# Eight array tiles and two PSUM pairs for the first step of an inverse transform, absolute phases on ScalarE, a joined table product, and a new order of all pieces

## The chip, the cores and the metric

The kernel runs on one core of a Trainium2 chip. The core has a matrix engine (TensorE, in the profile PE for the matmuls and PEld for the loads of weights), a vector engine (VectorE, DVE), a scalar engine (ScalarE, ACT), a general engine (GpSimd, POOL) and a queue that issues transfers (SyncE, SP). Each engine takes its own instructions strictly in the order in which the program lists them, and waits on semaphores for the others. TensorE writes its results to PSUM, from where ScalarE or VectorE must take them away before the place is used again; this is called evacuation here. The metric is the device time of one execution in microseconds (us), lower is better.

## What is computed

Two independent parts, whose results stand side by side in the output (2048 rows, 576 columns each):

```python
def _A_ref(x, wqkv, wo):                # sliding-window attention, 32 heads of 18, window 256
    qkv = (x @ wqkv).reshape(B, S, 3, H, Dh).transpose(2, 0, 3, 1, 4)
    q, k, v = qkv[0], qkv[1], qkv[2]
    scores = jnp.einsum("bhqd,bhkd->bhqk", q, k) * (Dh ** -0.5)
    mask = (idx[:, None] - idx[None, :] >= 0) & (idx[:, None] - idx[None, :] < W)
    p = _softmax(jnp.where(mask[None, None], scores, -1e9), axis=-1)
    return jnp.einsum("bhqk,bhkd->bhqd", p, v).transpose(0, 2, 1, 3).reshape(B, S, D) @ wo

def _B_ref(u, A_re, A_im, B_re, B_im, C_re, C_im, log_dt, Dskip):   # state-space convolution
    dt = jnp.exp(log_dt)[:, None]
    P = jnp.exp((dt * A)[:, :, None] * l[None, None, :])            # A = A_re + 1j A_im, 128 states
    K = jnp.einsum("dn,dnl,dn->dl", Cc, P, dt * Bc).real            # 2048 taps for each of 576 channels
    Yf = rfft2(pad(u)) * rfft2(pad(K))                              # transforms of length 4096
    return irfft2(Yf)[..., :L] + u * Dskip
return jnp.concatenate([a, b], axis=-1)
```

## The kernel before

**Stages.** The front loads x and the weights, scales them, splits each into a high and a low half-precision part and starts the projections. The tables stage computes, for 18 groups of 32 channels, the factors of exp(dt A l) from exponentials and sines, multiplies them into two tables (P and Q) and forms the taps K from these on TensorE (L615), then K's first transform step (L631, L635) and u's (L493); the projections to q, k and v (L204) run between these. Then come the attention of 16 items (4 blocks of rows by 4 groups of heads) and the convolution's remaining steps side by side, and at the end the output product with wo.

**Pieces and their order.** The work is cut into pieces, each a stream that a letter names. A string of letters for each stage, `PLAN`, sets the order of the pieces; a letter with a digit is the follow-up of a piece (an evacuation, a store). Nothing is rescheduled after that: each engine gets its instructions in the order in which the pieces are written. The letters that matter here are G (factors and phases to PSUM, L505, and folding them, L511 and L514), N (sines), R (products for P, on GpSimd), M (exponentials and Q), X (taps), P (projections), s (score blocks whose maxima VectorE takes, L906, L914 and L940), a (scores for the softmax, L982, and their exponential, L1000), v (product with V, L1020), c (spectra of the convolution, L718), d (the first step of the inverse transform, L752), e (its last step, L815) and w (output product).

**The ring.** PSUM has three places of two banks each, the ring pairs. Most pieces on TensorE take one, c takes two, v none (it has its own, `po`). A second string, `SLOTS`, says which pair comes next. A piece that takes a pair waits until the evacuation of its last user is done, and so does everything behind it in TensorE's queue.

**Inverse, first step.** 24 steps (3 channel groups by 8). Each has 16 fp32 matmuls of 32 rows, 64 columns of weights and 192 streamed columns; the trace counts two for each, 768 in all. b numbers four row groups of 32. Row group b writes to column half b % 2 of one pair, so four different tiles of the array are used in turn. One ScalarE instruction (L759) evacuates the pair, two stores of 128 partitions bring it to `h` in DRAM, from where the last step (L815) reads it once eight inverses are done.

**Phases.** `fold` subtracts from a phase its whole part (L514) and, with an integer AND on VectorE (L515), writes its absolute value beside it, for the cosine. `t_sin` takes sine and cosine on ScalarE (L556, L557, L561, L562). `t_q` forms Q by four VectorE products of 512 elements (L601 to L604).

Of the kernel before, what the change touches and what calls it, by code (L numbers as in the profile page):

```python
# [29 lines left out]
HC = GC // 2  # L30
# [12 lines left out]
def constants():  # L43
# [23 lines left out]
    for nm, v in mult.items():  # L67
# [25 lines left out]
        "P2U4X1XMGPMGX5G5RP1PG6M1PP2X2PP4NRPP4RPMP1MG1PP2PM1UX4PP1XGRX1NP4XG2PP2GX1MG5UX4G5MPG6U2G6X4P4RU1U4R"
        "P1M1X4XX2PPXMRNU4P2GPX5P1X1MNRP2PXG1G2P4PGM1X1PG5PPXP5X4GPPP5RX5UMG5G6PG6UPPNU1UX2MRRPP4U2M1U4UU2XPP"
        "5MMRX1PGP5P6UG1U1PM1PPPG2P5UX4NRU1PMPMGM1XPP5PX1U2RU4G5P5GG5PPG6RMGXG6PP5PRX2NP6NP4PPG1MG2XPPGX5PRM1"
        "UP1G5P2P1MMGX1M1G5G6P2G6X4RXX4PPX1NXPPGP1X2PX5MGP4X4XG1RRP2MPX1PG5PNM1RG2G6XP1GX1PG5P1MMM1XG6X2P2X4P"
        "X4GPP4PRRP2P4NNMX5XG1RMP1M1G2PP4PX1UU1P2PRMGG5P1PGU4XU2P4G5UMG6P2PP6PUPG6X1X4PPM1XNU1RP1PGMP4PMPRX5P"
        "2U2G1RXPP1M1UNP4X1P5PXPGUX1PU1X2PG5X4P5GU4P2MRPU4G2MPPX4G5PP5U2XPG6PG6U4RP6M1PMNXP6GPPMRP4PGNRPRX5P5"
        "G1GPZX2X1G2M1P5P5PX4G5PPP5G5XX4X1MGUPG6G6PXRX5MPM1PP5X2PXNMPMPP1PP2X4PG1M1UX1PRU1RG2MP4NU2GP1UXUG5X1"
        "MPU1G6M1RP4U4P1GP2PPPUPG5U2XPPP2G6RNMP1RUX5PX4GPG1X4X2P1P4P2U2RUP4MP4NG2XM1X4RPU1GPX1G5P2MXP1GMX1G5G"  # L100
        "6P2PP4G6PPM1RPU4U4PMP4NP1XX4X4XMPZX2ZPM1UP2PURRX5NGX1MU1U2P1MXPPP1GPPP2X4PM1G1X1GP2PPG5XU4P6P5PP5X4P"
        "MG5G2G6UUX5PRRPPG6P6URU2MNXX2RU1PPP5P4GX4M1P5U2U1X1NG1MP4PMPXGP6M1PPP6P5PG2MPX4PRG5PGMPPP5X1G6P5XRXG"
        "5M1P4G6P6RsP5P6NU4sX2P6sU4sRMs2ss2ssX5ss2X4ssZs2s2sss2s2s2Zs2ZX1Ns2ss2sXs2s2X1ss2Rss2XZs2s",
    "first":
        "s6X5s4sX2s2sX4s2RMsss2M1saaRs2Xa1ssa1s2X1MRXs2X1sXX4saas2aX5sas2sX2X4sa1sa1s2vX4s2vs2a1ss2X4s2s2ss2s"
        "s2aavsa1sssa1s",
    "rest":
        "s6s2asssa1s2s2s2s4va1s2ssvs2akLs2svss2skss2vLvksa1sks2vvv1as2ala1s2s2s2sas2s2aa1svcvsaa1a1as6snsasvc"
        "1cac6a1s4s2ss2va1ks2a1kLas2c2ks2c1asva1vsa1asa1vlc3s2caa1s2vc2svc1ks2vs2saa1dscc6as2c2sa1kc3sv1d1vc1"
        "c6asa1kLLs2ln3s2s2c2dln1a1c3cs2anss2vsad4d1c1vs2Lka1sasa1avsc6n3ss6n6s2d4Lvskva1ac3vvs2s4sa1ks2ss2Lc"  # L110
        "6dLn1s2s2saa1vvasd1d4s2da1salsssac2a1ks2svd1Laa1sv1s2d4s2slvs2s2s2s2s2sc3s2a1csa1sLdlas6cvasvsac1d1k"
        "sa1c2vc6vs2asnsc1ks4aa1sn4a1vs2ss2a1vas2s2a1d4ka1svsc3Ln6s2n4s2as2svLs2dsas2sc2cs2as2La1sc6s2v1s2vd1"
        "a1n3c3sadsc1a1s2ad4a1c2c6c3vs2vd1aa1kdsaslsvvd4nsaa1sd1s6vsa1kLad4kn3s2ss2a1svs4sssa1vs2vcn1s2ss2s2L"
        "s2asn6ass2ac1a1va1ffa1ss2s2Las2s2Ls2ses2s2c6a1sc2av1ve1c3a1vks2skssds6e4an4n1svasas2vss2d1ls2ss2s2a1"
# [24 lines left out]
    "2101201201210210201210210210212012021020121020120120120210210210212010212012012012012021021012102102"  # L139
    "0102102102012012012010210210120120120210210201201201201210210201201201201201201201201201202102102101"  # L140
    "2012012010210210120120121021021021021021020120120120210120120102102102102102120120120120121200201201"
    "202010210210200210210212012"
)


# [1127 lines left out]
```

## Time and profile before

| | |
|---|---|
| Runs (us) | 786.18, 777.06, 781.0; median 781.0 |
| Profiled execution, first to last instruction | 784.5 us; its time is not listed apart from that |
| Mean granted TensorE clock | 0.963 |
| Busy, share of the span | PE 88%, DVE 75%, ACT 68%, POOL 53% |
| Front | 0 to about 53 us |
| Tables | to about 345 us, last taps end at 382.5 us |
| First inverse, last inverse | 421.0 us, 717.0 us |

A row of the profile that groups instructions reads: line, engine, operation, tiles out<-in, shapes, count | busy time in us, mean ns of one | idle time of the engine just before them, and what ended it. A row of waits reads: who <- for whom: us in total, times, longest. In the chain of waits a row is start, length, what. L752 is line 752 of the kernel before. A matmul's duration in the trace includes its way through the array, which the next one overlaps.

### The profile page before, as it was taken

What the parts mean: (1) busy time and instruction counts of PE and PEld (TensorE: products, weight loads), DVE (VectorE), ACT (ScalarE), POOL (GpSimd) and SP (SyncE); (2) the same over time, 40 slices, a digit from 0 to 9 for tenths busy, and PEclk for the clock granted to TensorE, in tenths of its full rate; (3) what the DMA queues carried; (4) which work ended last, traced back from release to release, by engine and by line L of the source; (5) the groups of instructions that cost most, each with busy time, mean ns of one, the idle gap of its engine ahead of it and who ended that gap; (6) DMA issues with size and microseconds to landing.
All of it is one profiled execution on the core that took longest, in us unless ns stands there. A gap on an engine that the chain in (4) does not pass through costs nothing.

```text
span 784.5 us, 29499 instructions
## 1 busy us (share of the span) xinstructions
PE 693.0 (88%) x12956; PEld 410.8 (52%) x12956; DVE 588.2 (75%) x779; ACT 534.3 (68%) x709; POOL 417.3 (53%) x309
## 2 busy tenths in 40 slices
PE   3786878998989989997789999989989998999997
PEld 2532444565545654665544555544555554557775
DVE  5998789998998897988777888876888586852100
ACT  2369577787887777773458677775877876786622
POOL 2245867987688666866007574451553444546120
PEclk9979799999999999996999999998999999899999
DMA  8998055738247537889578777676866786555786
GB/s 309 342 215 204 7 133 149 159 83 216 51 120 182 133 70 175 230 183 277 113 238 279 247 240 231 207 243 166 245 185 203 240 256 207 170 163 159 205 258 187
DMA packets 215904, 150.67 MB, mean 192 GB/s; under 512 B 103530, under 2 KB 195818, under 8 KB 215520
## 3 DMA queue, kind: packets, MB, share of 16 engines
q1 hardware_dynamic: 214160, 146.28, 66.0%
q0 software_dynamic: 1616, 2.52, 1.1%
q8 instruction: 101, 1.65, 0.8%
q14 instruction: 27, 0.22, 0.1%
HBM read 83.50 MB, written 65.11 MB: 189 GB/s over the span
## 4 chain that ended last, share of the span: by engine, by line
PE 55%; DVE 17%; ACT 15%; issue 6%; DMA 4%; SPq 1%; POOL 0%; ACTq 0%; DVEq 0%
PE po L1020 9%; PE pp L204 9%; PE ring L204 7%; PE ring L906 5%; DVE m L940 5%; PE ring L752 4%; PE ring L982 4%; PE ring L615 4%; PE ring L718 4%; PE ring L505 2%; DMA wraw<-in_wr_dram 2%; DVE amx L192 2%; PE ring L815 2%; ACT raw L1000 2%; DVE wl L372 2%
## 5 line engine op out<-in xcount | busy, mean ns | idle before, releaser
L940 DVE TENSOR_REDUCE m<-ring 128x2 f32<-128x640 f32 (+4 forms) x256 | 190.8, 779 | 66.0 <-PE ring L914 58.2
L586 POOL TENSOR_TENSOR m<-A,tr 128x1024 f32<-128x1024 f32 x72 | 141.5, 1983 | 52.6 <-DVE m L592 43.5
L1000 ACT ACTIVATE P<-ring,esc 128x1024 f32<-128x1024 f32 (+2 forms) x86 | 90.0, 1060 | 37.1 <-PE ring L995 32.7
L1000 ACT ACTIVATE raw<-ring,esc 128x1024 f32<-128x1024 f32 (+2 forms) x74 | 77.2, 1061 | 19.4 <-PE ring L995 18.8
L734 POOL TENSOR_TENSOR t<-X 128x768 f32<-128x768 f32 x24 | 46.7, 1944 | 76.1 <-ACT X L726 75.6
L1063 POOL TENSOR_TENSOR oh<-osb,oh 128x1024 f16<-128x1024 f32 x16 | 34.1, 2133 | 59.5 <-ACT oh L1059 42.9
L914 PE MATMUL ring<-sm,idb 64*64 64x128 bf16 x896 | 56.1, 224 | 3.3 <-issue 3.1
L204 PE MATMUL pp<-xh,wh 128*128 128x512 f16 x180 | 48.1, 397 | 10.0 <-DVE qst L453 5.0
L204 PEld LDWEIGHTS <-wh 128*128 128x128 f16 x324 | 30.7, 99 | 49.1 <-issue 11.7
L615 PE MATMUL ring<-Q,m 128*32 128x64 f32 x2304 | 42.9, 231 | 12.8 <-ACT fa L511 4.1
L1055 POOL TENSOR_TENSOR osb<-osb,T 128x1024 f32<-128x1024 f32 x16 | 38.6, 2410 | 25.8 <-DVE T L1050 23.8
L592 DVE TENSOR_TENSOR m<-m,m 128x1024 f32<-128x1024 f32 x36 | 51.6, 1432 | 0.7 <-POOL m L586 0.6
L615 PEld LDWEIGHTS ring<-Q,m 128*32 128x32 f32 x2304 | 36.9, 117 | 27.2 <-ACT mab L547 5.5
L906 PEld LDWEIGHTS <-raw 54*64 54x64 f16 x704 | 28.6, 108 | 41.1 <-issue 37.7
L740 POOL TENSOR_TENSOR Y<-t,t 128x384 f32<-128x384 f32 x24 | 24.7, 1029 | 46.1 <-DVE t L734 33.8
L906 PE MATMUL ring<-K,raw 54*64 54x320 f16 (+4 forms) x576 | 44.8, 308 | 4.5 <-ACT raw L1000 0.8
L204 PE MATMUL pp<-xh,wl 128*128 128x512 f16 x180 | 48.0, 400 | 0.6 <-DVE wl L372 0.6
L567 POOL TENSOR_TENSOR tr<-tr,mab 128x768 f32<-128x768 f32 x18 | 33.3, 1850 | 28.4 <-ACT tr L562 28.4
L726 ACT ACTIVATE X<-ring 128x768 f32<-128x768 f32 x48 | 36.7, 812 | 14.3 <-PE ring L718 8.1
L995 PE MATMUL ring<-tm,idb 64*64 64x256 bf16 (+2 forms) x640 | 45.0, 257 | 0.0
L982 PEld LDWEIGHTS <-K 55*64 55x64 f16 x1280 | 28.8, 108 | 26.7 <-issue 22.7
L752 PE MATMUL ring<-Y,i 32*64 32x192 f32 x768 | 38.7, 336 | 3.3 <-issue 2.3
(171 smaller groups left out, 1725.1 us busy)
## 6 DMA issues: line engine op xcount, KB each, us to landing
gk<-kst SPq DMA_DIRECT2D x36, 256.0 KB
gx<-ust SPq DMA_DIRECT2D x16, 576.0 KB
xk<-gx SPq DMA_DIRECT2D x24, 384.0 KB
xk<-gk SPq DMA_DIRECT2D x24, 384.0 KB
h<-ho SPq DMA_DIRECT2D x48, 192.0 KB
hp<-h SPq DMA_DIRECT2D x24, 384.0 KB
K<-kz SPq DMA_DIRECT2D x14, 512.0 KB
raw<-qz SPq DMA_DIRECT2D x11, 512.0 KB
```

The source lines that it names most:

```text
L204: self.nc.tensor.matmul(ps, u, v, start=(i == 0), stop=(i == len(ops) - 1))
L586: tt(m[part], A[:, ch, a0:a0 + 8].unsqueeze(3).to_broadcast(sh), tr[:, ch, part, 0:8].unsqueeze(2).to_broadcast(sh), op=OP.mult)
L592: self.nc.vector.tensor_tensor(m[0], m[0], m[1], op=OP.add)
L615: nc.tensor.matmul(kp[32 * st:32 * st + 32, j, :], m[:, ch, 32 * term:32 * term + 32], Q[:, ch, term, :], start=(term == 0), stop=(term == ...
L734: mul(ts[i], X[:, :, :, :192].rearrange("p i s j -> p s i j"), X[:, i, :, 192:].unsqueeze(2).to_broadcast(sh), op=OP.mult)
L752: nc.tensor.matmul(ps[64 * (b % 2):64 * (b % 2) + 64, b // 2, 192 * s:192 * s + 192], self.i1[32 * b:32 * b + 32, t, o:o + 64], Y[32 * b:3 ...
L906: nc.tensor.matmul(ps[z:z + 64, b, :n], d["Q"][rr, 2 * b + pp, 64 * qb:64 * qb + 64], d["K"][rr, 2 * b + pp, k0:k1], start=True, stop=Fals ...
L914: nc.tensor.matmul(out, self.idb[rr], self.sm[rr], start=False, stop=True, skip_group_check=True)
L940: self.nc.vector.tensor_reduce(out, x, axis=AX.X, op=OP.max)
L982: nc.tensor.matmul(ps[z:z + 64, b, off:off + w], d["K"][rr, 2 * b + pp, kc:kc + 64], d["Q"][rr, 2 * b + pp, q0:q0 + w], start=(k == 0), st ...
L1000: nc.scalar.activation(P[:, :, lo:hi], ps[:, :, lo:hi], AF.Exp, scale=self.esc)
L1020: nc.tensor.matmul(po[32 * p:32 * p + 32, z, q0:q0 + w], V[64 * z:64 * z + 64, kb * 76 + 19 * p:kb * 76 + 19 * p + 32], P[p % 2][64 * z:64 ...
```

## The change

Four edits. The first spreads the inverse's matmuls over eight tiles: the column half is now the transform's half s, the four row groups write to four banks, and so two ring pairs are taken; two ScalarE instructions evacuate them, and the two stores read 64 partitions each. The second takes the absolute value of a phase out of `fold` and lets ScalarE do it in `t_sin`. The third joins two of the four products of `t_q`. The fourth replaces all strings of `PLAN` and `SLOTS` (751 ring pairs instead of 727, one more for each inverse).

```diff
 PLAN = {
     "front":
-        "AAAVCACAAAAAVAVVV1CV1CAVAVAAVCAV1ACCVCACCVVV1VV1CVCACBBPABV1CCPV1BV1CPCPP1PVP2PP4CPAPP1PP2BPCP1P4BVP"
+        "AAAAAAAAAAAAAAAAACCCCCCCVCCCCVBVV1V1AVVVV1CV1CVVVBV1AVBBCV1CVCPCVV1PAV1CVCVBBC",
...
         def sub():
             nc.vector.tensor_tensor(k, x, k.bitcast(I32), op=OP.subtract)
-            nc.vector.tensor_scalar(f[:, 1].bitcast(I32), k.bitcast(I32), 0x7FFFFFFF, None, op0=OP.bitwise_and)
             self.n[end] += 1
...
             f = self.fr[c]
+            nc.scalar.activation(f[:, 1], f[:, 0], AF.Abs)
             nc.scalar.activation(f[:, 0], f[:, 0], AF.Sin, scale=-TWO_PI)
...
         v = lambda z: z.rearrange("p (c m) -> p c m", m=12)
+        nc.scalar.activation(f[:, 1], f[:, 0], AF.Abs)
         nc.scalar.activation(tr[:, :, 1, :], v(f[:, 0]), AF.Sin, scale=TWO_PI)
...
-        tt(Q[:, :, 0, 32:64], cs, m[:, :, 32:64], op=OP.mult)
+        tt(Q[:, :, :, 32:64], f.rearrange("p i (c m) -> p c i m", m=32)[:, :, ::-1],
+           m[:, :, 32:64].unsqueeze(2).to_broadcast([128, HC, 2, 32]), op=OP.mult)
         tt(Q[:, :, 0, 0:32], cs[:, :, ::-1], m[:, :, 0:32], op=OP.mult)
-        tt(Q[:, :, 1, 32:64], sn, m[:, :, 32:64], op=OP.mult)
...
     def inverse(self, n):
         nc, (ch, t), Y = self.nc, divmod(n, 8), self.Y.pop(n)
-        ps = self.slot()
-        for s in range(2):
-            for i in range(2):
-                for b in range(4):
+        ps = [self.slot() for _ in range(2)]
+        for i in range(2):
+            for b in range(4):
+                for s in range(2):
                     o = (2 * s + i) * 64
-                    nc.tensor.matmul(ps[64 * (b % 2):64 * (b % 2) + 64, b // 2, 192 * s:192 * s + 192],
-                                     self.i1[32 * b:32 * b + 32, t, o:o + 64], Y[32 * b:32 * b + 32, i, s],
-                                     start=(s == 0 and i == 0), stop=(i == 1), skip_group_check=True)
+                    nc.tensor.matmul(ps[b // 2][64 * s:64 * s + 64, b % 2, :192], self.i1[32 * b:32 * b + 32, t, o:o + 64],
+                                     Y[32 * b:32 * b + 32, i, s], start=(i == 0), stop=(i == 1), skip_group_check=True)
...
         def go():
-            ho = self.p["fs"].tile([128, 2, 2, 192], F32, name="ho")
-            nc.scalar.activation(ho.rearrange("p s b j -> p b s j"),
-                                 ps[:, :, :384].rearrange("p b (s j) -> p b s j", s=2), AF.Copy)
+            ho = self.p["fs"].tile([128, 4, 192], F32, name="ho")
+            for k in range(2):
+                nc.scalar.activation(ho[:, 2 * k:2 * k + 2], ps[k][:, :, :192], AF.Copy)
...
             for s in range(2):
-                nc.sync.dma_start(v[t, s], ho[:, s])
+                f = 8 * t + 4 * s
+                nc.sync.dma_start(self.h[f:f + 4, :, :, 192 * ch:192 * ch + 192].rearrange("b a l j -> (a l) b j"),
+                                  ho[64 * s:64 * s + 64])
...
-            yield "PE", lambda: (self.Y[n],), "ring", lambda: n in self.Y
+            yield "PE", lambda: (self.Y[n],), "ring", "ring", lambda: n in self.Y
             self.inverse(n)
```

Three places show the new order, in rows of the built program (line, operation, tile written <- tiles read, shape, count; lines from 180 to 600 stand one or two lower after the change). The first is on TensorE where an inverse is followed by a spectrum, ahead of the change:

```order
L914 LDWEIGHTS idb
L914 MATMUL ring<-sm,idb 64x2x64
L752 MATMUL ring<-Y,i_5189 64x192 x16
L718 MATMUL ring<-xk,w_5188 32x384 x16
L982 LDWEIGHTS K_4695
L982 MATMUL ring<-Q_4696,K_4695 64x256
```

and such a place after it:

```order
L995 LDWEIGHTS idb
L995 MATMUL ring<-tm,idb 64x128
L1020 MATMUL po<-P,raw 32x320 x8
L752 MATMUL ring<-Y,i_5231 64x192 x16
L718 MATMUL ring<-xk,w_5230 32x384 x16
L922 MATMUL ring<-idf,m 32x128
L906 LDWEIGHTS raw
```

The inverse has as many matmuls as before; a product with V (L1020), which takes no ring pair, stands ahead of it here and of ten others. Inverse and spectrum together now take four pairs, not three.

The second is ScalarE in the tables, around the first sines (fr and fa hold the phases, qst a projection, mab and ring exponentials), ahead of the change:

```order
L511 ACTIVATE fa<-ring 128x384
L527 ACTIVATE ring<-ring 128x1024
L511 ACTIVATE fr<-ring 128x512
L556 ACT_TABLE_LOAD
L556 ACTIVATE fr<-fr 128x512
L557 ACTIVATE fr<-fr,halfpi 128x512
```

and after it:

```order
L510 ACTIVATE fa<-ring 128x384
L449 ACTIVATE qst<-pp 128x512 x2
L525 ACTIVATE ring<-ring 128x1024
L510 ACTIVATE fr<-ring 128x512 x2
L554 ACTIVATE fr<-fr 128x512
L555 ACT_TABLE_LOAD
L555 ACTIVATE fr<-fr 128x512
L556 ACTIVATE fr<-fr,halfpi 128x512
```

The absolute value (L554) stands ahead of each pair of sine and cosine, and two evacuations of projections now stand ahead of the exponential.

The third is TensorE at the end of the tables, where the first score blocks (L906 and L917) run. Ahead of the change one block follows the other:

```order
L917 LDWEIGHTS idb
L917 MATMUL ring<-sm,idb 64x64
L906 LDWEIGHTS raw
L906 MATMUL ring<-raw 64x192
L906 LDWEIGHTS raw
```

and after it four matmuls of a projection to v (L203, in its own PSUM place pp) stand between two blocks here:

```order
L917 LDWEIGHTS idb
L917 MATMUL ring<-sm,idb 64x64
L203 LDWEIGHTS xl
L203 MATMUL pp<-wh,xl 128x288
L203 LDWEIGHTS xl
L203 MATMUL pp<-wh,xl 128x288
```

In all, 74 projection matmuls stand behind the first score block now, and none did.

More of the change, by code (lines that the diff above doesn't have):

```diff
@@ L93 @@
[L93 to L102, printed above, removed]
@@ new lines @@
+        "G1G2XX1GG5G6GG5G6NRMPPPM1MRX4X4X4U4NXX5X2UUP4P4P2U1U2UPU4XP1P4X1UMRRPU2X4X4PM1XX1P5P2PU1PMGPP5PG1G2X"
+        "GX5G5G6MPX2X4PM1UNRGP5G5P6MRPPPPPRX4G6UU2NP5P6P4XPX1RXP5PMM1MPU1PP5PX1PPGGGG5U4G6G1G2NG5G6PPXX2P5PPR"
+        "RMM1X5MMM1PPP5XNMMPP1P2RX1RGG1NPPPP1G2GG5RM1G6UXX1GMMPPG5G6XX2P6PP2PRXM1NX1RX5GNPMMP1P2GM1RG5G6PG1PP"
+        "4P4P1GG5G6P4X4X4P2PG2NXX1MPRPURU2PU1P1XP2XX4X4P4RX5X2X4RGG1P4NG2PMX1XM1X1GMP1P2MM1G5G6UPGG5G6NRRPPPP"
+        "1XP4X2PXPRMP1MP2X1PX5RM1UP2NPPP1U4U2U4GPPPX4X4G1MP5U1G2GGG5P2G5G6G6PRMM1RPPP5X4XX1P4MRPPPPPUUU2XX2NU"
@@ new lines @@
+        "1UU4U4P5X5PP5GG1XX1MM1G2PPPPP5MPGPPG5G6P6P5MM1PPGG5G6X4PRPP5X4PPXX1NRXX2NPX5MRPPUU1U2UUU2U4X4P5MM1XU"
+        "1RX1GRMGG5G6G1G2PGPP4P1P2G5PPG6P4P4UUU2NNUXX1U1PPXRU4U4RX2RP6UZP1X5P2ZU2RGG1G2PU1MM1MMXPX1PP1P2GGM1M"
+        "G5G6G5PPPMG6P4P4XP1P2PNRRRPP1P2ZZM1MX4X1XNX2PMP4PP4P1XX1X5X4RXGPPG1M1X4X1G2XX5MX2P1P6ZGG5P2P4GG5NRG6"
+        "G6MM1PPMPP2RUUU4NU1U2PPX4XP1X1X4RRUUU2U1GGP2MG1M1G2NX4X4PP1XX1G5PPMMM1PG6XRP2PPX5RP5XPX2P5MGPG5PX1RG"
+        "6ss2ss2Nsss2s2ss2P4sP4sP4s2s2U4U4Pss2sssP5s2Ps2Ps2ss2ss2PssPPPRP6P6P6P5P6s2s2MM1ss2MMPP5X4PXPM1MX1XP"
@@ new lines @@
+        "1saa1kvs2c2avva1aa1ss2cc1ss2s4asvva1ss2saa1vs2vks2ckc3v1c2c6LLkksc3s2c1ada1d1ndd1cc2c6c3sc1as2Lsss6v"
+        "d4a1s2ac2da1d4d1ss2ava1sasa1s2s2ks4aa1c6c3kLcc1c6ss2ss2kvss2aa1aa1c2vvc3vsss2cc1ss2ss2s2avla1dd1sc6a"
+        "vkc2ka1s2svs2sd4s2aLss2LLsn6vv1va1aa1s2ss6sLss2s2dd4d1ssss2s2s2csn3n1s2c1ac3c2a1c6aaa1ss2a1vaa1ss2av"
+        "sa1sks2s2akka1vvssc3s4s2aaa1a1sLs2Ls2ass2a1lcc1c6ss2vvc2dn6d1aLa1ss2aa1vc3sas6sss2d4va1s2ksaa1ss2s2s"
+        "s2vv1dd1kkdd4d1s4cd4c1nn3ss2aa1vd4ssc2vs2s2c6c3aa1svaa1s2ssvvan4n1s2s2a1ssvvn4s2s2ssaLLs2vsvs2s2aLa1"
@@ L139 @@
[L139 to L142, printed above, removed]
+    "0120201012010210212021201212012010202120212010210121122010210200120221021201212012102012010102111200"
+    "0122012012102001022120121011202102022101210121020212021002102010022021021012012002121021021021021021"
@@ new lines @@
+    "0212020120120120102102102102120121012012012012012012012102012010120120120120120120120120102102102010"
+    "2102102102102102102012012012102012102102102102102102101202102102102120212012012012012012012012102102"
+    "1202102102102102102102101201202102100210210210210210210120120120120120120210120121021021201202102102"
+    "1021210210210210210210120120120120120120210210201201202102102012012101201201201201201021201201201202"
+    "1021021012012102102010210210120120120120120120102102101201201201210210210212012102102120120102102021"
@@ L143 @@
+    "021021021010210210210102102101021021021021021020210"
 )
```

59 lines of the change are left out of this document (24 added, 35 removed).

## The prediction

> **What bounds the kernel now.** I read the page first (busy time, the chain of waits), then the busy time by stage, then the groups of the lines that the change touches.
>
> ```profile
> span 784.5 us, 29499 instructions
> ...
> PE 693.0 (88%) x12956; PEld 410.8 (52%) x12956; DVE 588.2 (75%) x779; ACT 534.3 (68%) x709; POOL 417.3 (53%) x309
> ...
> PE 55%; DVE 17%; ACT 15%; issue 6%; DMA 4%; SPq 1%; POOL 0%; ACTq 0%; DVEq 0%
> ```
>
> TensorE is busy 88% of the span, and it holds 55% of the chain that ended last; VectorE and ScalarE hold 17% and 15%. By stage (front, tables, the end of the tables, attention with convolution, the tail):
>
> ```profile
> core 0: us, PE busy (x) PEld busy (x) DVE busy (x) ACT busy (x) POOL busy (x), PEclk, DMA share, GB/s
> 0.00:53.00 53.00, 32.44 (x117) 18.36 (x118) 42.17 (x50) 19.91 (x26) 12.33 (x20) 0.90 0.92 300
> 53.00:345.00 292.00, 258.23 (x3382) 148.31 (x3381) 255.20 (x343) 226.75 (x360) 218.15 (x169) 0.97 0.58 140
> 345.00:402.00 57.00, 45.52 (x1051) 31.43 (x1058) 48.21 (x76) 25.43 (x39) 20.76 (x18) 0.85 0.75 196
> 402.00:700.00 298.00, 276.98 (x7336) 155.33 (x7321) 231.06 (x300) 225.15 (x243) 143.21 (x92) 0.98 0.73 222
> 700.00:784.50 84.50, 79.79 (x1082) 57.39 (x1080) 11.51 (x14) 37.04 (x44) 22.88 (x13) 1.00 0.64 196
> ```
>
> From 402 us on TensorE is the bound: 356.77 us busy of 382.5. What it no longer has to do there comes off the span, as long as nothing new makes it wait. In the tables (53 to 345) it is nearly level with VectorE, 258.23 against 255.20, and ScalarE is not far below with 226.75.
>
> **The inverse step (L752).** It removes no matmul; it spreads the same ones over eight array tiles instead of four. The neighbouring spectrum step (L718) already fills eight.
>
> ```profile
> L752 PE MATMUL ring<-Y,i 32*64 32x192 f32 x768 | 38.7, 336 | 3.3 <-issue 2.3 <-POOL oh L1063 0.4 <-DVE m L940 0.3
> L718 PE MATMUL ring<-xk,w 64*32 64x384 f32 x768 | 38.6, 487 | 0.8 <-DVE m L940 0.7
> ```
> ```profile
> L752 PE MATMUL ring<-Y,i x768: 317/321/576, 421.0 to 716.7; 32*64 32x192 f32 x192
> ```
> ```profile
> L718 PE MATMUL ring<-xk,w x768: 479/482/508, 406.5 to 708.6; 64*32 64x384 f32 x192
> ```
>
> Both have 768 matmuls and the same busy time (38.7 and 38.6 us), though those of L718 stream twice the columns: eight at once with 384 columns cost what four at once with 192 do. The medians give the streaming alone: 482 less 321 ns is 161 ns for 192 columns, so 160 ns of each matmul is latency. An inverse has 32 matmuls: eight waves of four now, 8 x 161 = 1.29 us and the latency; four waves of eight then, 0.64 us and the latency. That is 0.64 us less for each of 24 inverses, 15.5 us, all on TensorE after 402 us, where it is the bound. From below the price is nothing saved (the two column halves of one row group run one after the other); I take 15.5, since L718 runs eight tiles with four on the same rows.
>
> A row on small matmuls bears on this: 64 of them took 1.10 us here, 17 ns each, under the 20 ns that an inverse of 0.64 us needs.
>
> ```profile
> 167.39 1.10 PE ring L615 x64
> ```
>
> The Trainium skill, "TensorE: Matmul & The Clock Gate", section on the 56 ns gap, states that starts of matmuls never come closer than about 25 ns. By that an inverse would take 32 x 25 = 0.80 us and the 24 would save 11.8 us. The trace of this case does not agree (17 ns), so the row decides.
>
> **Its second PSUM pair.** The inverse now takes two of the three ring pairs and writes both at once, so it waits until the step before the last one has been evacuated. Nothing in the trace shows this step with two pairs; the nearest is L718, which takes two. Four waves of 2 x 161 ns and 160 ns of latency are 1.45 us; its busy time is 38.6 / 24 = 1.61, so about 0.16 us each is lost, 3.9 us in 24. From above the price is the whole gain, 15.5 us, since L718 fills its first pair for 0.64 us before it needs the second and the inverse does not; from below 0. I take 3.9: the new order puts matmuls of L1020, which need no ring pair, ahead of many inverses.
>
> Behind a waiting inverse stands all of TensorE's queue, score and projection matmuls alike, and behind those ScalarE and VectorE.
>
> **Its evacuation.**
>
> ```profile
> L759 ACT ACTIVATE ho<-ring 128x768 f32<-128x768 f32 x24 | 19.5, 811 | 16.7 <-PE ring L752 16.6
> ...
> L547 ACT ACTIVATE mab<-ring 128x384 f32<-128x384 f32 x18 | 8.8, 491 | 2.2 <-PE ring L505 2.1
> ```
>
> One evacuation of 811 ns becomes two of 128x384, by L547 491 ns each: 0.17 us more, 4.1 us in 24. ScalarE is busy 225.15 of 298 there and holds 15% of the chain: 0.6 us on the path (0 to 4.1). The stores to h stay 48 of 192 KB in SyncE's queue, from 64 partitions instead of 128: I cost that at nothing, because the reads of h come only after eight inverses of a channel group.
>
> **Absolute phases and the joined product, in the tables.**
>
> ```profile
> L592 DVE TENSOR_TENSOR m<-m,m 128x1024 f32<-128x1024 f32 x36 | 51.6, 1432 | 0.7 <-POOL m L586 0.6
> ...
> L515 DVE TENSOR_SCALAR fr<-fr 128x512 int32<-128x512 int32 x36 | 35.7, 992 | 1.2
> ...
> L601 DVE TENSOR_TENSOR Q<-fr,ring 128x512 f32<-128x512 f32 x36 | 24.5, 680 | 7.6 <-ACT ring L527 4.9 <-PE ring L615 2.0 <-ACT fr L557 0.7
> ...
> L556 ACT ACTIVATE fr<-fr 128x512 f32<-128x512 f32 x36 | 22.4, 623 | 0.4 <-DVE fr L515 0.2
> ...
> L515 DVE TENSOR_SCALAR fa<-fa 128x384 int32<-128x384 int32 x18 | 13.2, 733 | 0.6
> ...
> L514 DVE TENSOR_TENSOR fa<-ring,fa 128x384 f32<-128x384 f32 x18 | 9.9, 551 | 8.1 <-ACT fa L511 8.0
> ...
> L561 ACT ACTIVATE tr<-fa 128x384 f32<-128x384 f32 x18 | 9.1, 507 | 0.0
> ```
>
> VectorE loses 35.7 + 13.2 = 48.9 us. ScalarE gains an Abs for each; no row shows one, and by the Sin of the same shapes (L556, L561) it is 22.4 + 9.1 = 31.5 us. The built program has 37 table loads before and after. The joined product has 1024 elements: by L601 and L514, which read PSUM too, 128 more elements cost 129 ns, so 680 + 4 x 129 = 1.20 us for two of 0.68, 0.16 us less, 5.8 us in 36; by L592 (1432 ns, both operands in SBUF) it would be 2.6 us more. I take 5.8 less. VectorE then falls by 54.7 of 255.2 us, 21%, and ScalarE rises by 31.5 of 226.75, 14%. What that is worth is read from what TensorE waits for in this stage; these six rows are the longest:
>
> ```profile
> PE pp L204 <- DVE qst L453: 6.0, 6, 2.2
> PE ring L615 <- ACT fa L511: 4.1, 1, 4.1
> PE ring L615 <- DVE fa L514: 2.5, 3, 1.4
> PE ring L505 <- DVE fr L514: 2.3, 3, 1.7
> PE pp L204 <- DVE xh L385: 2.1, 2, 1.2
> PE ring L505 <- ACT kst L647: 2.1, 3, 1.2
> ```
>
> 12.9 us name VectorE and 6.2 ScalarE. In proportion that is 2.7 us less and 0.9 more, together 1.8 us off. The bounds: all 12.9 gone, or all 31.5 of ScalarE on the path; I take the proportion, since neither engine alone is ahead in these rows by as much as the load moves.
>
> **The new order.** At the end of the tables TensorE now does 74 projection matmuls between the first score blocks; before it did none there. One costs 13.35 / 108 = 0.124 us by the same kind of matmul in the tail, so 9.2 us of work.
>
> ```profile
> 749.01 13.35 PE ring L204 x108
> ```
>
> They stand where TensorE was idle 57 - 45.52 = 11.5 us, and where its clock fell:
>
> ```profile
> 360.00:380.00 20.00, 15.31 (x347) 11.07 (x350) 17.61 (x32) 5.57 (x7) 11.72 (x11) 0.67 0.72 206
> ```
>
> They come out of the middle of the tables, so part of the hole may only move there; between 0 and 9.2 us I take half, 4.6 off. Scores of one more item move into the tables with their maxima on VectorE (0.78 us each, in the room made there) and one store of a maximum on SyncE; the loads of the first two items move forward in SyncE's queue, past projections' stores that were not on the chain. In the front, two products (this one, L330, and its twin L331) now stand ahead of the first split of x on VectorE:
>
> ```profile
> 45.21 0.75 DVE L330 TENSOR_TENSOR x<-C_re,B_re 128x576 f32<-128x576 f32 x1
> ```
>
> That makes the first projections up to 1.5 us later (0 if the factor matmuls put between cover it); VectorE was full there, so I take 1.4. In the tail, where TensorE is busy 79.79 of 84.5 us, I take nothing: what stands behind the last L1020 is the same output products and last steps, two of each more.
>
> **Sum** on the profiled span: 784.5 - 15.5 + 3.9 + 0.6 - 1.8 - 4.6 + 1.4 = 768.5 us. The median of the runs, 781.0, is 0.4% below that span (777.06 to 786.18 lie around it), so the forecast is 768.5 x 781.0 / 784.5 = 765 us. What is likely late next is ScalarE, in the tables.
>
> **Rivals.** All are in the same measure.
> - Waits for the second pair give the gain back. If each inverse waits the 0.64 us that L718 can hide and it can't, 15.5 us are lost instead of 3.9: 777 us, no change that counts. For it: in the new order two inverses and a spectrum follow each other directly in two places, six pairs in a row. Against it: L718 lost 0.16 us. The Trainium skill, "TensorEngine Tiling (Array Packing)", PSUM Bottleneck, speaks for this rival: tiling makes TensorE faster, not the evacuation, which may become the bound. The runs of before do not show that here.
> - The tiles don't overlap. Then the streaming of an inverse stays at 1.29 us: 768.5 + 15.5, 780 us. L718's rows speak against it.
> - Slower: ScalarE sets the pace of the tables. With 226.75 + 31.5 it stands at 258.3 us, exactly TensorE's 258.23, in a strict order with the evacuations that TensorE waits for. If none of the 31.5 us is hidden, the time is 768.5 - 0.9 + 31.5, 795 us. It decides (over 1% slower) from 25 us of the 31.5 on. Against it: ScalarE is idle 292 - 226.75 = 65 us in this stage.
> - A larger gain: VectorE was the real brake of the tables, and half of TensorE's 33.8 idle us there goes, 16.9 instead of 1.8: 753.4, 750 us.
>
> **Chances.** The forecast 0.58 (its own range 756 to 773); the larger gain 0.12; waits for pairs 0.14; no overlap 0.04; ScalarE 0.12. About 1% is what a measurement of this kernel can tell from no change, 773 to 789 us. Faster by more: 0.58 + 0.12 = 0.70. Within: 0.14 + 0.04 = 0.18. Slower: 0.12. From 748 to 783 us the range holds all but ScalarE's case and a little below.
>
> **What would show it.** Right: L752 at about 23 us busy instead of 38.7 with as many matmuls; its evacuations near 491 ns; L515 gone from VectorE and Abs on ScalarE at 0.5 to 0.63 us; the last taps (L615) some 3 to 7 us earlier than at 382.5 us. Wrong: L752 still near 38 us, or waits of L752 on ScalarE's and VectorE's evacuations that add up to 10 us; TensorE waiting for ScalarE in the tables for more than 20 us, or taps that end later than now.

## The result, and the profile after

The changed kernel is slower: 806.97 us, median of four runs (798.10 to 811.54), against 779.03 us for four runs of the kernel before; the ratio is 1.030, 95% interval 1.021 to 1.038. The forecast was 765 us, in a range of 748 to 783. The profiled execution is the longest of the four, 811.54 us, with a span of 809.8 us; the ratio leaves that run out.

The page of the changed kernel, first its span, the busy time of the engines and the chain that ended last:

```profile
span 809.8 us, 29546 instructions
...
PE 685.3 (85%) x12956; PEld 390.7 (48%) x12956; DVE 561.0 (69%) x689; ACT 564.5 (70%) x787; POOL 417.0 (51%) x309
...
PE 43%; DVE 19%; ACT 14%; DMA 10%; issue 8%; SPq 3%; POOL 2%; ACTq 0%; DVEq 0%; POOLq 0%
```

TensorE has less work than before (685.3 for 693.0 us) in a longer span, and its share of the chain fell from 55% to 43%: it waits more. VectorE is down by 27 us, ScalarE up by 30.

To see where, both spans are cut at 53 us, about where the front ends, and at the same two events, the end of the last taps (L615) and the end of the last score maximum (L940). The kernel before, then the changed one, in busy time by window:

```profile
53.00:383.00 330.00, 288.52 (x4035) 170.48 (x4033) 288.80 (x395) 245.20 (x389) 238.91 (x186) 0.95 0.60 147
383.00:707.00 324.00, 299.21 (x7814) 169.71 (x7815) 249.39 (x327) 236.04 (x256) 146.46 (x93) 0.98 0.72 217
707.00:785.00 78.00, 72.79 (x998) 52.26 (x995) 7.79 (x9) 33.12 (x39) 19.64 (x11) 1.00 0.66 204
```
```profile
53.00:391.00 338.00, 287.15 (x4053) 165.50 (x4051) 256.37 (x309) 269.51 (x442) 238.97 (x186) 0.97 0.57 139
391.00:718.00 327.00, 281.75 (x7656) 147.43 (x7648) 250.62 (x321) 230.41 (x266) 140.39 (x89) 0.98 0.69 209
718.00:810.00 92.00, 85.28 (x1169) 58.61 (x1153) 12.41 (x13) 43.72 (x56) 26.77 (x16) 0.99 0.71 210
```

The tables take 8 us more, with the same work on TensorE and 32 us less on VectorE. The stage with attention and convolution has 158 matmuls and 17.5 us of TensorE's work less, and still takes 3 us more. The tail has 171 matmuls more and takes 14 us more. The granted clock (the last column but two) does not explain it: it is within 0.02 of before in each window.

Work has moved from the stage with attention into the tail, so the two are best taken together. From the last taps to the end, the kernel before and the changed one:

```profile
382.50:784.50 402.00, 372.25 (x8817) 222.03 (x8817) 257.40 (x336) 269.55 (x296) 166.09 (x104) 0.98 0.71 215
```
```profile
390.70:809.80 419.10, 367.33 (x8809) 206.14 (x8809) 263.04 (x333) 274.42 (x321) 167.16 (x104) 0.98 0.69 209
```

TensorE is busy 4.9 us less there and idle 51.8 us instead of 29.8. That idle time is what has to be explained.

The groups of the inverse in the changed kernel show that the edit itself did what it says:

```profile
L752 PE MATMUL ring<-Y,i 32*64 32x192 f32 x768 | 26.4, 335 | 3.0 <-issue 1.1 <-ACT P L1000 0.9 <-ACT ho L758 0.3
...
L758 ACT ACTIVATE ho<-ring 128x384 f32<-128x384 f32 x48 | 21.1, 488 | 17.7 <-PE ring L752 13.4 <-DMA h<-ho 2.2 <-DMA Q<-m 1.1
```

The same 768 matmuls are 26.4 us busy instead of 38.7, 12.3 us less, and an evacuation takes 488 ns, where 491 were expected. A single inverse that nothing holds up, in the kernel before and in the changed one:

```profile
427.10 1.53 PE L752 MATMUL ring<-Y,i 32*64 32x192 f32 x32
```
```profile
552.38 0.91 PE L752 MATMUL ring<-Y,i 32*64 32x192 f32 x32
```

It is 0.62 us shorter. TensorE waits for neither pair for long (L758 0.3 us, L1000 0.9 us in this row). So the new waits are elsewhere. In the stage with attention, TensorE's longest waits (engine, line, what was waited for: us in total, times, longest) are:

```profile
PE po L1020 <- issue: 13.4, 10, 2.3
PE ring L906 <- DVE m L940: 4.3, 14, 0.7
PE ring L906 <- DMA K<-kz: 4.2, 2, 3.2
PE ring L982 <- DVE m L940: 3.9, 9, 1.3
```

Over all rows of this query the waits add up to 42.3 us (391 to 718 us) against 22.0 us before (383 to 707): "issue" 20.5 for 9.6, maxima on VectorE 10.5 for 5.4, loads of K 4.2 for nothing. That is 20.3 us more, against 17.5 us less work: the 3 us.

"Issue" means that the profile shows nothing that the engine waited for. The timeline at one such stop in the middle of a step of L1020:

```profile
527.76 0.36 PEld L1020 LDWEIGHTS po<-raw,V 64*32 64x32 f32 x20
527.76 0.52 PE L1020 MATMUL po<-raw,V 64*32 64x128 f32 x19
...
530.52 0.87 PE L1020 MATMUL po<-raw,V 64*32 64x64 f32 x29 [2.25 <-issue]
530.52 0.28 PEld L1020 LDWEIGHTS po<-raw,V 64*32 64x32 f32 x28 [2.40 <-issue]
```

Both halves of TensorE stand still for over 2 us in the middle of a step, with no wait that the profile shows. The page's table of DMA queues has a queue that carries instructions:

```profile
q8 instruction: 101, 1.65, 0.8%
```

101 packets of 16 KB for the 26,036 records of TensorE (matmuls, weight loads, semaphore waits): one packet for about 256 of them. Counted in order of start, the five stops of L1020 that are longer than 1.7 us before 705 us come after record 14,529, 18,113, 20,673, 21,953 and 22,977. Each of these leaves 193 when divided by 256: they stand at the same place of a block of 256. And at each a packet of that queue lands just after TensorE ran dry:

```
block  TensorE at    its packet     and    TensorE's 256   packet   stop, us
       record 193    starts after   takes  records take    late by
55     523.8 us      4.15 us        0.99   4.22            0.92     2.46
69     594.0         4.15           1.02   4.27            0.90     2.22
84     677.0         4.15           0.97   3.99            1.14     2.51
88     698.0         3.96           0.91   3.87            1.00     2.52
```

The next block is fetched from about record 193 of the block before on (67 of the 69 packets behind 383 us start after it; this is inferred). From 383 us on the packet starts 1.9 us later in the median, 3.8 us in the worst tenth, and takes about 1 us; TensorE uses a block up in 4.9 us in the median, and in 3.9 to 4.3 in these four blocks, which hold runs of L1020's steps. Where the packet's delay and duration together are longer than that, it stops, and goes on about 1.4 us after the packet is in. Counted in this way (time between the starts of the two records, where a packet lands when TensorE has run dry, or within 0.15 us of it) the changed kernel has 8 such late blocks, 16.7 us; the kernel before has 3, 6.0 us.

That is not all. At other boundaries the packet lands a little before TensorE has run dry, and TensorE still goes on only 1.2 to 1.7 us after the landing. With these short stops (all boundaries behind the last taps with more than 0.25 us between the two starts) the changed kernel has 22 stops, 28.2 us, and the kernel before 17, 14.4 us.

### The profile page after: what moved, and what is told of

Read it like the earlier page. It is cut to its first block, busy times and chain, and to the rows that moved or that the text cites. A ratio compares the mean times of both kernels' runs of the same rounds, so it can differ in the third digit from the quotient of the medians.

```text
span 809.8 us, 29546 instructions
## 1 busy us (share of the span) xinstructions
PE 685.3 (85%) x12956; PEld 390.7 (48%) x12956; DVE 561.0 (69%) x689; ACT 564.5 (70%) x787; POOL 417.0 (51%) x309
## 4 chain that ended last, share of the span: by engine, by line
PE 43%; DVE 19%; ACT 14%; DMA 10%; issue 8%; SPq 3%; POOL 2%; ACTq 0%; DVEq 0%; POOLq 0%
PE po L1020 8%; PE ring L203 6%; DVE m L940 6%; PE pp L203 6%; PE ring L906 4%; PE ring L982 3%; PE ring L718 3%; DMA wraw<-in_wr_dram 2%; PE ring L752 2%; PE ring L615 2%; DMA K<-kz 2%; DMA qz<-qst 2%; ACT raw L1000 2%; DVE t L734 2%; PE ring L815 2%
## 5 line engine op out<-in xcount | busy, mean ns | idle before, releaser
L940 DVE TENSOR_REDUCE m<-ring 128x2 f32<-128x640 f32 (+4 forms) x256 | 188.7, 778 | 66.4 <-PE ring L914 62.1
L1000 ACT ACTIVATE P<-ring,esc 128x1024 f32<-128x1024 f32 (+2 forms) x86 | 89.4, 1060 | 39.8 <-PE ring L995 36.7
L1000 ACT ACTIVATE raw<-ring,esc 128x1024 f32<-128x1024 f32 (+2 forms) x74 | 76.5, 1062 | 28.8 <-PE ring L995 28.3
L592 DVE TENSOR_TENSOR m<-m,m 128x1024 f32<-128x1024 f32 x36 | 59.0, 1640 | 3.3 <-POOL m L586 1.9
L601 DVE TENSOR_TENSOR Q<-fr,ring 128x1024 f32<-128x1024 f32 x36 | 43.8, 1217 | 20.3 <-ACT ring L525 15.6
L914 PE MATMUL ring<-sm,idb 64*64 64x128 bf16 x896 | 54.0, 220 | 1.9 <-issue 1.9
L203 PE MATMUL pp<-xh,wh 128*128 128x512 f16 x180 | 47.5, 393 | 9.0 <-DVE xh L384 7.5
L203 PEld LDWEIGHTS <-wh 128*128 128x128 f16 x324 | 31.3, 99 | 49.1 <-issue 16.8
L906 PE MATMUL ring<-K,raw 54*64 54x320 f16 (+4 forms) x576 | 45.1, 313 | 10.7 <-DMA K<-kz 4.2
L567 POOL TENSOR_TENSOR tr<-tr,mab 128x768 f32<-128x768 f32 x18 | 34.7, 1926 | 32.7 <-ACT tr L562 32.6
L615 PE MATMUL ring<-Q,m 128*32 128x64 f32 x2304 | 41.1, 225 | 11.5 <-DVE m L592 5.5
L906 PEld LDWEIGHTS <-raw 54*64 54x64 f16 x704 | 26.8, 106 | 46.8 <-issue 43.2
L203 PE MATMUL pp<-xh,wl 128*128 128x512 f16 x180 | 47.8, 398 | 0.0
L615 PEld LDWEIGHTS ring<-Q,m 128*32 128x32 f32 x2304 | 35.4, 113 | 23.6 <-issue 6.8
L740 POOL TENSOR_TENSOR Y<-t,t 128x384 f32<-128x384 f32 x24 | 24.6, 1024 | 42.1 <-DVE t L734 33.3
L982 PEld LDWEIGHTS <-K 55*64 55x64 f16 x1280 | 29.4, 107 | 32.6 <-issue 29.5
```

What stands on the lines that cost most here:

```text
L203: self.nc.tensor.matmul(ps, u, v, start=(i == 0), stop=(i == len(ops) - 1))
L592: self.nc.vector.tensor_tensor(m[0], m[0], m[1], op=OP.add)
L615: nc.tensor.matmul(kp[32 * st:32 * st + 32, j, :], m[:, ch, 32 * term:32 * term + 32], Q[:, ch, term, :], start=(term == 0), stop=(term == ...
L906: nc.tensor.matmul(ps[z:z + 64, b, :n], d["Q"][rr, 2 * b + pp, 64 * qb:64 * qb + 64], d["K"][rr, 2 * b + pp, k0:k1], start=True, stop=Fals ...
L914: nc.tensor.matmul(out, self.idb[rr], self.sm[rr], start=False, stop=True, skip_group_check=True)
L940: self.nc.vector.tensor_reduce(out, x, axis=AX.X, op=OP.max)
```

## The experiments

Twelve kernels. In the diffs, "order of before" and "new order" are the two versions of PLAN and SLOTS; the three edits of the code (inverse, absolute phases, joined product) and the order together are exactly the change.

**The edits in the order of before.** SLOTS gets one entry more for each inverse (of the other two pairs, the one that comes free first), PLAN stays.

```diff
-            nc.vector.tensor_scalar(f[:, 1].bitcast(I32), k.bitcast(I32), 0x7FFFFFFF, None, op0=OP.bitwise_and)
...
+            nc.scalar.activation(f[:, 1], f[:, 0], AF.Abs)
...
-        tt(Q[:, :, 0, 32:64], cs, m[:, :, 32:64], op=OP.mult)
...
-        ps = self.slot()
+        ps = [self.slot() for _ in range(2)]
```

> The kernel before with all three edits of the code (inverse on eight tiles over two ring pairs, Abs on ScalarE, joined product) in the order of before; only the second pair of each inverse is added to the table of pairs. If the new order is what costs the time (theory A), this is faster than before: 760 to 772 us against 779. If the edits cost it (theory B: ScalarE's Abs in the tables, or waits for the second pair), it is near the changed kernel: 795 to 810 us.

Measured: 826.18 us, ratio 1.058 (1.054 to 1.062). Neither: the edits cost more in the order of before than the whole change does.

**The new order with the code of before.** The entries of the second pairs are taken out of SLOTS.

```diff
-        "AAAVCACAAAAAVAVVV1CV1CAVAVAAVCAV1ACCVCACCVVV1VV1CVCACBBPABV1CCPV1BV1CPCPP1PVP2PP4CPAPP1PP2BPCP1P4BVP"
...
+        "AAAAAAAAAAAAAAAAACCCCCCCVCCCCVBVV1V1AVVVV1CV1CVVVBV1AVBBCV1CVCPCVV1PAV1CVCVBBC",
...
```

> The code of before in the new order (the entries of the inverse's second pair are taken out of the table of pairs). Theory A (the order costs): slower than the changed kernel by what the edits save, 812 to 825 us. Theory B (the edits cost): near before, 775 to 788 us.

Measured: 840.89 us, ratio 1.075 (1.069 to 1.080). Theory A in sign, but by more than it said. 34.6 us are lost by the end of the last taps (417.1 us instead of 382.5), where GpSimd waits 80.9 us for VectorE's sums (L592 of before) instead of 43.5; it may be that the new order needs the work taken off VectorE. Order and code belong together: each alone is worse than both. (This table of pairs, too, was made by a rule and not planned anew.) So the order is not simply bad: with it the edits cost less than without, and the question becomes what each edit breaks.

**Abs alone,** in the order of before.

```diff
-            nc.vector.tensor_scalar(f[:, 1].bitcast(I32), k.bitcast(I32), 0x7FFFFFFF, None, op0=OP.bitwise_and)
...
+            nc.scalar.activation(f[:, 1], f[:, 0], AF.Abs)
...
+        nc.scalar.activation(f[:, 1], f[:, 0], AF.Abs)
```

> The kernel before with Abs on ScalarE as its only edit, in the order of before. Forecast's own term (VectorE 2.7 us of waits less, ScalarE 0.9 more): 774 to 782 us, last taps within 4 us of 382.5. ScalarE as the bound of the tables: 788 us or more, last taps at 390 us or later.

Measured: 808.93 us, ratio 1.035 (1.030 to 1.040); the last taps end at 405.5 us instead of 382.5. ScalarE as the bound, and more than its 788 us. The waits in the tables, of the kernel before (53 to 383 us) and of this one (53 to 406 us; its L568 and L563 are L567 and L562 of before):

```profile
POOL tr L567 <- ACT tr L562: 28.4, 14, 7.9
DVE fa L514 <- ACT fa L511: 8.0, 6, 2.8
...
DVE qst L453 <- ACT qst L450: 5.2, 7, 1.7
DVE fr L514 <- ACT fr L511: 4.9, 5, 1.3
```
```profile
POOL tr L568 <- ACT tr L563: 62.9, 17, 9.5
...
DVE fa L514 <- ACT fa L511: 24.7, 10, 5.1
...
DVE qst L453 <- ACT qst L450: 19.0, 11, 3.3
DVE fr L514 <- ACT fr L511: 17.4, 19, 3.2
```

VectorE does not use the time it was given: three of its steps wait for ScalarE 61.1 us instead of 18.1, behind sines that now take an Abs longer. GpSimd's wait for the sines more than doubles. ScalarE is busy 271.98 of 353 us there, so 77%; that it had idle time was no protection, because what the others wait for stands behind the longer block in its queue.

**The inverse alone,** in the order of before.

```diff
-        ps = self.slot()
+        ps = [self.slot() for _ in range(2)]
...
+            for k in range(2):
+                nc.scalar.activation(ho[:, 2 * k:2 * k + 2], ps[k][:, :, :192], AF.Copy)
```

> The kernel before with the inverse on eight tiles over two pairs as its only edit, in the order of before. L752 was 12.3 us less busy in the changed kernel (26.4 for 38.7). If TensorE keeps what it is spared: 765 to 771 us. If waits for the second pair eat it: 776 to 783 us. L752 should be busy 26 to 27 us in both cases.

Measured: 801.58 us, ratio 1.026 (1.022 to 1.030), above both expectations; the last taps end at 383.7 us, so nearly all of it is lost behind the tables. L752 is 33.3 us busy, not 26 to 27. TensorE's waits (384 to 801 us):

```profile
PE ring L906 <- ACT ho L758: 9.7, 12, 1.6
PE ring L982 <- ACT ho L758: 3.6, 5, 1.0
PE ring L752 <- DVE m L940: 3.3, 7, 1.0
PE ring L752 <- ACT raw L1000: 2.6, 4, 0.8
...
PE ring L922 <- ACT ho L758: 2.1, 2, 1.2
...
PE ring L752 <- ACT P L1000: 1.4, 3, 0.6
```

All rows with L758 add up to 17.9 us: the score step behind an inverse needs a pair, and both are still full. The other rows of L752 with an evacuation add up to 8.1: the inverse itself waits until two pairs are empty. 26.0 us of waits (1.4 us in the same rows of the kernel before) for 5.4 us of work saved. (The table of pairs was lengthened by a rule and not planned anew; a better one may wait less.)

**Two pairs, four tiles.** The same pairs, evacuations and order as in the run before, with the matmuls of the kernel before; as there, both pairs are finished in the last waves.

```diff
-        for s in range(2):
-            for i in range(2):
+        for i in range(2):
+            for s in range(2):
                 for b in range(4):
...
-                    nc.tensor.matmul(ps[64 * (b % 2):64 * (b % 2) + 64, b // 2, 192 * s:192 * s + 192],
+                    nc.tensor.matmul(ps[s][64 * (b % 2):64 * (b % 2) + 64, b // 2, :192],
```

> The order of before; the inverse takes two pairs and two evacuations of half the size, as in the run with the inverse alone, but its matmuls stay on four tiles (both pairs are finished in the last waves, as with eight). If the second pair is what costs: idle TensorE around L752 about as there (23 us), L752 near 38.7 us busy, 803 to 812 us. If the eight tiles themselves cost (TensorE slower, not waiting): 779 to 786 us.

Measured: 802.29 us, median of 800.80, 802.29 and 810.77 (a fourth run took 1278.42), ratio 1.029 (1.021 to 1.038). L752 is 42.1 us busy, and the same rows name the evacuation (14.4 us with that of the inverse, 8.0 in the other rows of L752). So it is the second pair with its two evacuations that costs, not the eight tiles.

**No absolute value at all,** in the order of before and in the new order; the cosine is taken of the signed phase.

```diff
-            nc.scalar.activation(f[:, 1], f[:, 0], AF.Abs)
...
-            nc.scalar.activation(f[:, 1], f[:, 1], AF.Sin, scale=-TWO_PI, bias=self.halfpi)
+            nc.scalar.activation(f[:, 1], f[:, 0], AF.Sin, scale=-TWO_PI, bias=self.halfpi)
```

> The kernel before without any absolute value (the cosine is taken of the signed phase: that part of the computation is left out), order of before. It tells what taking the 48.9 us off VectorE is worth by itself. The forecast's term was 2.7 us: 775 to 780 us. If VectorE was the real brake of the tables (rival 'larger gain'): 767 us or less.

Measured: 780.73 us, ratio 0.997 (0.993 to 1.001). Taking 48.9 us off VectorE is worth at most a few us, and by the interval perhaps nothing. The run with Abs alone differs from this one by ScalarE's 31.5 us of Abs: 808.93 less 780.73 is 28 us, and its last taps end 23.6 us later.

> The changed kernel without any absolute value (left out as in the run before). It tells what Abs on ScalarE still costs in the new order. If the new order hides it: 802 to 808 us, last taps within 3 us of 390.7. If the 8.2 us that the tables lost are Abs: 796 to 800 us, last taps at 380 to 384. If ScalarE is the pace there as it was in the old order (23 us for 31.5 us of Abs): 780 to 790 us.

Measured: 799.46 us, ratio 1.024 (1.017 to 1.031), and the last taps at 383.4 us instead of 390.7. Of the 8.2 us that the changed kernel lost in its tables, 7.3 are Abs on ScalarE; the new order hides most of it, but not all. And without it nothing is gained over the 382.5 us of before. This rests on one profile of each: the ratio's interval overlaps that of the changed kernel.

**The joined product alone,** in the order of before.

```diff
+        tt(Q[:, :, :, 32:64], f.rearrange("p i (c m) -> p c i m", m=32)[:, :, ::-1],
+           m[:, :, 32:64].unsqueeze(2).to_broadcast([128, HC, 2, 32]), op=OP.mult)
```

> The kernel before with the joined product as its only edit, order of before. VectorE loses about 5 us of its work in the tables (0.14 us in 36 steps). After the run without absolute values, where 48.9 us less on VectorE were worth nothing that could be measured: 779 to 784 us, the same as before. If the shorter step sits on the chain of each table (Q then taps): 5 us less, 775 to 778 us.

Measured: 781.53 us, ratio 1.003 (0.999 to 1.006): the same. Its profile has no late block and 6.1 us of short stops, and a span of 775.1 us.

**The boundaries of the instruction blocks, moved.** 32 or 64 small matmuls, overwritten by the real ones, go to the front of TensorE's queue; nothing else changes. The expectations count 64 and 128 instructions, but each of these matmuls leaves four records (two matmuls and two weight loads), so that the traces hold 128 and 256 more. The first moves every boundary by half a block; the second by a whole block, which leaves the boundaries at their old places in the program.

```diff
                 ps.append(self.p["pp"].tile([128, 512], F32, name="pp")[:, :288])
+                for k in range(32 if tk + hf == 0 else 0):
+                    nc.tensor.matmul(ps[hf][:32, :16], x[:32, 0, :32], w[:32, 0, 1152:1168], start=True, stop=False, skip_group_check=True)
                 for k in range(4):
```

> The changed kernel with 64 more instructions (32 small matmuls, overwritten by the next one) at the front of TensorE's queue, so that every later boundary of its 256-instruction blocks lies 64 instructions earlier in the program. If the stops of 1.5 to 2.5 us in runs of L1020 are late instruction blocks: they stand at the boundaries of the blocks again, in other places of the program, and their sum is another than 16.7 us (0 to 20 us), with the time from the last taps to the end changed by as much. If they belong to the places (an unseen wait of L1020): the same places of the program, the same sum.

Measured: 797.6 us, two runs, ratio 1.020 (1.012 to 1.028). Six late blocks, 9.3 us, in other places of the program (two in L1020's steps, four elsewhere); with the short stops 21.6 us instead of 28.2. From the last taps to the end it takes 409.0 us instead of 419.1. The places themselves are the control: at the 69 places where the changed kernel has its boundaries, the times between the two starts add up to 29.5 us there and to 1.2 us here, where the boundaries lie half a block away. So the boundary costs the time, and not the step that stands there. That this kernel is faster than the changed one is not shown, since the two intervals overlap.

> The changed kernel with 128 more instructions at the front of TensorE's queue. If runs of L1020 and the DMA load make blocks late wherever the boundary falls: stops of 9 to 17 us again, more than in the order of before, 796 to 808 us. If it was the luck of one alignment: under 5 us of stops, 790 to 796 us.

Measured: 808.94 us, ratio 1.038 (1.031 to 1.046). Eleven late blocks, eight of them in L1020's steps, 19.8 us and so above the 17 that were expected. As the boundaries are at their old places, this is no third alignment but the changed kernel's once more, and all eight of its late blocks are late again, at the same places. The new order has many stops with either alignment.

> The kernel before with 64 more instructions at the front of TensorE's queue and nothing else. Late instruction blocks cost 6.0 us in its profile (3 stops). If their places are chance: the sum is another one, 0 to 12 us, and the time follows it, 774 to 788 us; the stops stand at the boundaries of the blocks, not at the three places of before.

> As the run before, with 128 instructions: a third place of the boundaries. Sum of the stops 0 to 12 us, time 774 to 788 us, and over the three kernels the order of the times is the order of the sums.

Measured: 791.76 us, ratio 1.016 (1.009 to 1.022), with 4 late blocks, 8.4 us; and 788.36 us, ratio 1.010 (1.002 to 1.018), with 3 late blocks, 4.9 us. The times are longer than expected and not in the order of the sums, since the added matmuls delayed the tables (last taps at 386.9 and 390.3 us). Behind the tables the order holds: 404.3, 402.0 (before) and 399.3 us for 8.4, 6.0 and 4.9 us of late blocks, or 18.5, 14.4 and 9.2 us of all stops. The second of the two has its boundaries where the kernel before has them, and still two of its three late blocks stand at other ones: where a boundary lies does not alone decide whether its block is late.

**All kernels side by side.** One profile each, in us: end of the last taps, from there to the end of the span, late blocks (number, time), all stops at boundaries of instruction blocks, and the third column less the time of all stops.

```
kernel                                last taps  to the end  late   us    all    us   rest
order of before, one pair
  before                                  382.5       402.0     3  6.0     17  14.4  387.6
  joined product                          385.0       390.1     0  0.0      9   6.1  384.0
  no absolute value                       381.9       397.4     3  5.2     11  10.6  386.8
  Abs on ScalarE                          405.5       397.9     2  3.7      9   9.9  388.0
  128 records more                        386.9       404.3     4  8.4     17  18.5  385.8
  256 records more                        390.3       399.3     3  4.9     10   9.2  390.1
order of before, two pairs
  inverse alone                           383.7       416.4     0  0.0      8   4.2  412.2
  two pairs, four tiles                   384.6       415.7     1  1.4      8   5.0  410.7
  all three edits                         407.3       417.3     0  0.0      6   3.4  413.9
new order, one pair
  code of before                          417.1       423.3     7 12.5     15  16.7  406.6
new order, two pairs
  changed kernel                          390.7       419.1     8 16.7     22  28.2  390.9
  no absolute value                       383.4       411.4     7 12.0     15  17.6  393.8
  128 records more                        388.9       409.0     6  9.3     21  21.6  387.4
  256 records more                        394.6       417.9    11 19.8     26  29.9  388.0
```

The last column falls into groups: 384 to 390 (order of before, one pair), 387 to 394 (new order, two pairs), 407, and 411 to 414. The stops explain most of what differs inside the first: its six kernels have 14 us between them from the last taps to the end, and 6 us without the stops. They also explain most of what parts the changed kernel from the kernel before: 17.1 us from the last taps to the end, and 3.3 us without the stops.

## Why the prediction was wrong

- **No new wait but the second pair's: this is the step that failed.** The prediction said that what TensorE no longer has to do behind the tables "comes off the span, as long as nothing new makes it wait", and its only new wait was 3.9 us for the second pair. For the time from the last taps to the end it so had 11.0 us less (15.5 less 3.9 and 0.6); measured are 17.1 us more. TensorE is idle 51.8 us there, not 29.8. Of the 28.1 us by which the two differ, 13.8 are stops at instruction blocks (28.2 us for 14.4), which stood in no term and no rival; 9.3 are waits for maxima (5.1 more) and for K (4.2 more); 3.2 are work that the inverse did not save; 1.8 are left over. Six of the changed kernel's eight late blocks stand in steps of L1020, which the new order puts in rows behind the inverses; in the order of before it is four of 16, over the nine kernels with it. The one stop of 2.3 us by "issue" on L752 was a late block, in a row that the prediction quoted, and it was not asked what it was.
- **Eight tiles, -15.5 us:** right in kind, and in size too where nothing holds the step up: 0.62 us less for an inverse, where the sum had 0.64. But only 8 of the 24 inverses run without a pause, and over all L752 is 12.3 us less busy. The 11.8 us by the 25 ns of the Trainium skill ("TensorE: Matmul & The Clock Gate", section on the 56 ns gap) come nearer to that by luck: the trace does not agree with 25 ns as the least distance of two starts, since the 32 starts of the inverse shown above lie within 0.585 us, 19 ns apart in the mean.
- **Second pair, +3.9 us:** right for the new order, where TensorE's waits for L758 and those of L752 for evacuations add up to 2.7 us. The reason given fits: steps of L1020, which need no pair, stand behind the inverses. In the order of before the same edit costs 26.0 us of waits, more than the rival's 15.5. What the sum lacked is that this cover has a price, below.
- **The new order as a set of single moves** (-4.6 for projections, +1.4 for the front, nothing for the tail): the tail was taken as unchanged, since "what stands behind the last L1020 is the same". It is 14 us longer, with 171 matmuls more, because steps of the convolution (the last inverse ends at 745.8 us, 29 us later than before) and output products come later; most of that is work moved out of the stage before. With the one-pair inverse the new order takes 406.6 us behind the tables without stops, where the order of before takes 384 to 390: by this one run, whose table of pairs was not planned anew, it costs some 17 to 23 us. With the two-pair inverse it takes 387 to 394, so the inverse brings back some 13 to 19, no less than the 15.5 less 3.9 of the sum. The inverse's gain was there, and the order that makes it possible costs as much or more.
- **VectorE in the tables, -2.7 us:** agrees: 0.3% of 783 us is 2.3 us, though the interval (0.993 to 1.001) does not tell it from nothing. "The larger gain" was wrong.
- **ScalarE in the tables, +0.9 us:** the second step that failed, wrong by a factor of about eight. The 31.5 us of work was right (L554 takes 22.4 us, as was taken from the sine). Its price was read from what TensorE waits for directly, 6.2 us in rows, and scaled with the load. But ScalarE held up VectorE and GpSimd, as the run with Abs alone shows (61.1 us of waits for 18.1, and 62.9 for 28.4), and those held up TensorE. In the order of before 24 to 28 of the 31.5 us lie on the path, in the new order about 7 (7.3 by the last taps, 7.5 by the medians, 806.97 less 799.46). The "slower" rival had this mechanism, with 795 us and a chance of 0.12; it was held to be unlikely by ScalarE's 65 us of idle time, which is no argument in a strict order.
- **Projections at the end of the tables, -4.6 us, and the front, +1.4:** the gain was not found, and the two were not measured apart. Without Abs the tables of the new order end at 383.4 us, those of the old one at 382.5.
- **Evacuation, +0.6 us:** its size was right (488 ns for 491); what it costs on the path no run shows by itself.
- **Joined product:** nothing on the path, as the proportion said.

On the profiled spans it adds up: 8.2 us by the end of the last taps (390.7 less 382.5), of which 7.3 are Abs; and 17.1 us behind it, of which 13.8 are stops at instruction blocks: 25.3, from 784.5 to 809.8 us. Shown by experiment are the share of Abs, the second pair's cost in the order of before, and that the stops belong to the boundaries of the instruction blocks. That they cost the span their full length is read from the table and not shown by a run of its own. Not settled is how much the stops cost in other executions: each kernel has one profile, the changed kernel's is of its longest run, and in the order of before five kernels with one pair and the boundaries in the same places have between 6.1 and 14.4 us of stops. Nor is it settled how the 17 to 23 us of the new order with one pair divide: the waits for maxima and for K are read from one profile, and no run took the convolution's delay by itself. Why a packet starts late is open too: the DMA engines are 69% busy in this stage, but no run changed their load. None of the kernels is clearly faster than the kernel before.

## What to carry to other kernels

In kernels whose engines follow one fixed order, an engine's idle time is no room: ask what stands behind the lengthened step in its queue and who waits for that, over two engines and not one. An edit and its order can only be judged together; run the edits in the old order and the new order with the old code, since the two runs tell what the order repairs and what that costs. Before two orders are compared to a per cent, count the stops at TensorE's instruction blocks in both, the short ones too: here they differ by 14 us, half of what the change costs.

## What the runs showed of the hardware

Behind the last taps, stops at the boundaries of instruction blocks took 3.4 to 29.9 us of spans of 775 to 840 us in these kernels, up to 3.1 us each. The Trainium skill, "Runtime: NRT & Kernel Launch", section "Instruction fetch mechanics", says that instructions come in blocks of 16 KiB, 256 instructions, and that crossing a boundary is mostly hidden. The size agrees (101 packets of 16 KB for 26,036 records). That it is hidden holds for 47 of the changed kernel's 69 boundaries behind the last taps; at the other 22 the stops add up to 28.2 us.

The eight-tile inverse took 0.91 us instead of 1.53 where nothing held it up. Over 24 steps it was 26.4 us busy in the new order and 33.3 in the order of before, where the second pair was waited for within the step, with the same 768 matmuls of 321 ns in the median. The sum of two products on VectorE (L592), untouched by the change, took 1432 ns before and 1640 after, 1631 without absolute values in the order of before, 1450 with the joined product alone; the runs do not tell why.
